# Retention with a gated linear unit: output stores on GpSimd's DMA queue, query loads on SyncE's

## The chip, the cores and the metric

The kernel runs on one core of one Trainium2 chip. A core has five engines that run side by side, each through its own instructions in order: TensorE (PE, matmuls and, as PEld, its weight loads), VectorE (DVE), ScalarE (ACT), GpSimd (POOL) and SyncE (SP, which here only issues transfers). Transfers between HBM and the on-chip memory (SBUF) run on 16 DMA engines; they are issued from SP, ACT or POOL. The metric is the device time of one execution in microseconds (us), lower is better.

## What is computed

Eight batches, eight heads, 576 tokens, head dimension 64, all inputs and the output in 32-bit floats:

```
scores = (q @ k^T) / sqrt(64)
ret    = (scores * Dmat) @ v             Dmat[i, j] = gamma_h^(i - j) for i >= j, else 0
x      = ret, heads side by side         8 x 576 x 512
gate   = sigmoid(sum_k conv_w[k] * x[t - 4 + k])     5 taps along the tokens, zeros before the start
out    = (gate * (x @ w_val)) @ w_out
```

## The kernel before

Tokens are taken in chunks of 128, so a batch has four full chunks and a tail of 64 tokens; the tails of two batches make one chunk. For each group of four batches there are sixteen full chunks and two tail chunks, 36 in all (`chunks`, numbered t). The decay is split into a factor for each token of v (`gin`) and one for each output token (`gout`), so that within a chunk a plain triangular mask suffices, and what earlier chunks contribute goes through a 64 x 64 state for each head.

The program is written out by hand as a loop over slots, t = -2 to 37 (line 419). The order of the lines in a slot is the order of instructions on each engine. A slot t

- issues the loads of chunk t + 6 on SP (`load`, lines 78 and 81: a 256 KB tile each of k and v, into 9 buffers each; a tail has its own q tile),
- casts to bf16 on POOL: v of chunk t + 2, multiplied by `gin` (`cast_v`, line 202), k of chunk t + 3 (`cast_k`, line 197), and one quarter of a batch's queries for the next slot (`cast_q`, line 215),
- on PE makes the scores of chunk t + 1 (line 260), the values of chunk t (line 301), transposes the keys of chunk t + 2 and that quarter of queries (line 222), and adds the carried part and the state's update of chunk t + 1 (lines 284 and 332); DVE masks the scores and copies the transposed keys out of PSUM (lines 269 and 230), ACT copies states and queries (lines 343 and 244),
- and does half of the second layer's unit n = t // 2 - 1, which is two chunks of x: an even slot does the convolution as matmuls (line 365), the sigmoid (ACT, line 373) and the value projection (line 380), an odd one the output projection (line 391), with ACT's copy of its result into `ob` (line 394, five buffers) and the store of it (lines 397 and 400).

So even slots are longer on PE than odd ones. From slot to slot the engines run apart as far as buffers allow: the bf16 tiles of k and v have four buffers each, those of q five.

A full batch's queries are loaded as one tile of 1 MB, `fqb`, of which line 215 casts a quarter (one remainder of the token number modulo 4) at a time. Batches 0 and 1 are loaded on SP at the start; batches 2 to 7 on POOL's queue, at the head of the slot that `qload` names, into three buffers. The quarters of batch b are cast in four slots that are placed backwards from the batch's first chunk (`qjobs`): for batches 2 to 7 the first of them is turned in slot 3, 7, 11, 17, 21 and 25, and cast one slot before that.

A store on SP waits for ACT's copy of its `ob`, and whatever SP has to load next waits behind it. The output weights are loaded as floats (`wof`, line 110) and cast to bf16 in slot 2: quarters 0 and 2 by DVE, 1 and 3 by ACT (line 190). The first output projection, in slot 3, is the first to need them.

The lines that the steps of the prediction follow:

```
for b in qload.get(t, []):           # line 438: query loads of a slot
    load_queries(b)
if t >= 0 and ok(t + LA - 2):        # line 440: k and v of chunk t + 6 on SP
    load(t + LA - 2)
```

Of the kernel before, what the change touches and what calls it, by code (L numbers as in the profile page):

```python
# [13 lines left out]
F32 = mybir.dt.float32  # L14
# [7 lines left out]
def kernel(  # L22
# [10 lines left out]
    nc = tc.nc  # L33
    B, H, S, D = q.shape
    DM = moe_w_val.shape[0]
    KC = moe_conv_w.shape[0]
    P = 128
    NP = H // 2
    NCH = S // P
    TAIL = S - NCH * P  # L40
    PAD = KC - 1
    GB = 4
    LA = 8
    RQ = NCH
# [5 lines left out]
    half = ctx.enter_context(tc.tile_pool(name="half", bufs=2))  # L50
# [13 lines left out]
    chunks = []  # L64
# [6 lines left out]
    with tc.manual_schedule():  # L71
# [13 lines left out]
        def load(t):  # L85
            kind, b, c = chunks[t]
            load_one("k", k, kind, b, c, LA + 1)
            if kind == "tail":
                load_one("q", q, kind, b, c, 2)
            load_one("v", v, kind, b, c, LA + 1)  # L90

        def load_queries(b):
            t = half.tile([P, H, RQ, D], F32, name="fqb", bufs=3)
            (nc.sync if b < 2 else nc.gpsimd).dma_start(out=t.rearrange("p h r d -> p h (r d)"),  # L94
                              in_=q[b, :, 0:RQ * P, :].rearrange("h (p r) d -> p h (r d)", r=RQ))
            loaded["qb", b] = t

# [85 lines left out]
        def prep_wv(copy, part):  # L183

            src = wvf.rearrange("p o (pr ab hl j) -> p o pr ab hl j", pr=2, ab=2, hl=2)
            for (blk, j0, ab, hl) in ((0, 0, 0, 0), (0, 64, 1, 0), (2, 0, 1, 1), (2, 64, 0, 1))[2 * part:2 * part + 2]:
                copy(wvb[:, :, blk:blk + 2, j0:j0 + 64], src[:, :, :, ab, hl, :])
# [7 lines left out]
        def cast_k(t):  # L195
            kb = bfp.tile([P, H, D], BF16, name="kb")
            (nc.vector if t < 2 else nc.gpsimd).tensor_copy(kb, loaded["k", *chunks[t]])  # L197
            kbf[t] = kb

        def cast_v(t):  # L200
            vb = bfp.tile([P, H, D], BF16, name="vb")
            nc.gpsimd.tensor_tensor(vb, loaded["v", *chunks[t]],  # L202
                                    gin[:, chunks[t][2], :].unsqueeze(2).to_broadcast([P, H, D]), op=ALU.mult)
            vbf[t] = vb
# [4 lines left out]
        def cast_q(job, eng=nc.gpsimd):  # L209
            qb = bfp.tile([P, H, D], BF16, name="qb", bufs=5)  # L210
            if job[0] == "own":
                src = loaded["q", *chunks[job[1]]]
            else:
                src = loaded["qb", job[1]][:, :, job[2], :]
            eng.tensor_copy(qb, src)  # L215
            qbf[job] = qb
# [10 lines left out]
        def turn_k(t):  # L227
            ps = turned(kbf[t])
            kt = tp_sb.tile([P, NP, P], BF16, name="kt")
            nc.vector.tensor_copy(kt, ps)  # L230
            ktd[t] = kt

        def turn_q(job, copy=nc.scalar.copy, pool=None):
            ps = turned(qbf[job], pool)
            if job[0] == "own":
                qt = tp_sb.tile([P, NP, P], BF16, name="qt")
                qtd["own", job[1]] = qt
                dst = qt
            else:
                b, r = job[1:]  # L240
                if r == 0:
                    qtd["batch", b] = tp_sb.tile([P, NP, RQ, P], BF16, name="qtb", bufs=2)
                dst = qtd["batch", b][:, :, r, :]
            copy(dst, ps)  # L244
# [21 lines left out]
        def masks(t, i):  # L266
            m = mask_q if chunks[t][0] == "full" else mask_t
            p = pp.tile([P, NP, P], BF16, name=f"p{i}")
            nc.vector.tensor_tensor(p, sps[t][i], m.unsqueeze(1).to_broadcast([P, NP, P]), op=ALU.mult)  # L269
            pt[t, i] = p  # L270
# [65 lines left out]
        def take_state(t):  # L336
            kind, b, c = chunks[t]
            if kind != "full":
                return
            s = sbl[b % GB] if c == NCH - 1 else sbd[c % 2]  # L340
            for i in range(2):
                r = slice(i * 64, i * 64 + 64)
                nc.scalar.copy(s[r, :, i * 64:i * 64 + 64], st[b][r, :, i * 64:i * 64 + 64])  # L343
            state[b] = s
# [41 lines left out]
        def project(n, i):  # L386
            kind, b, c = chunks[2 * n]
            last = n == NT // 2 - 1
            o = ps_g.tile([P, DM], F32, name="g")
            for j in range(NP):  # L390
                nc.tensor.matmul(o, lhsT=zsb[n, j // 2][:, j % 2, i * P:(i + 1) * P], rhs=wob[:, j, :],  # L391
                                 start=(j == 0), stop=(j == NP - 1))
            ob = op_sb.tile([P, DM], F32, name="ob")
            nc.scalar.copy(ob, o)  # L394
            if kind == "full":
                c0 = (c + i) * P
                nc.sync.dma_start(out=out[b, c0:c0 + P, :], in_=ob)
            else:
                for j in range(2):
                    (nc.scalar if last and j else nc.sync).dma_start(out=out[b + 2 * i + j, NCH * P:S, :], in_=ob[j * TAIL:(j + 1) * TAIL])  # L400


        ok = lambda t: 0 <= t < NT
# [9 lines left out]
        qload = {}  # L413
        for b in range(2, B):
            first = min(s for s in qjobs if ("batch", b, 0) in qjobs[s])
            qload.setdefault(max(0, first - LA + 4), []).append(b)

        v_copy, g_copy, s_copy = nc.vector.tensor_copy, nc.gpsimd.tensor_copy, nc.scalar.copy
        for t in range(-2, NT + 2):
            n = t // 2 - 1  # L420
            unit = 0 <= n < NT // 2
            odd = t % 2 == 1
            jobs = qjobs.get(t, [])
            if t == -2:

                cast_k(0)
                turn_k(0)
                for s in sbl:
                    nc.vector.memset(s, 0.0)
                for r in range(RQ):  # L430
                    cast_q(("batch", 0, r), nc.vector if r % 2 else nc.gpsimd)
                cast_v(0)
                for r in range(RQ):
                    turn_q(("batch", 0, r), s_copy if r % 2 else v_copy, ps_g if r < 3 else None)
                warm = consts.tile([P, 1], F32, name="warm")
                nc.scalar.activation(warm, lsc, AF.Sigmoid)
                continue
            for b in qload.get(t, []):
                load_queries(b)
            if t >= 0 and ok(t + LA - 2):  # L440
                load(t + LA - 2)
            if ok(t + 2) and t == -1:
                cast_k(t + 2)
            if ok(t + 2):
                cast_v(t + 2)
            if t == -1:
                prep_wv(g_copy, 0)
            if ok(t + 3):
                cast_k(t + 3)
            for job in qjobs.get(t + 1, []):  # L450
                cast_q(job)
            if ok(t):
                take_state(t)
            if ok(t + 1):
                scores(t + 1)
                masks(t + 1, 0)
            if ok(t):
                values(t)
                if not odd:
                    take_x(t)  # L460
            if ok(t + 1) and not odd:
                masks(t + 1, 1)
            if unit and not odd:
                conv(n)
                gate(n, 0)
                gate(n, 1)
            if ok(t + 2) and not 1 <= t <= 3:
                turn_k(t + 2)
            if ok(t) and odd:
                take_x(t)  # L470
            if ok(t + 1) and odd:
                masks(t + 1, 1)
            if t == -1:
                prep_conv_weights()
            early = jobs if not 1 <= t <= 3 else []
            if unit:
                project(n, 0) if odd else value(n, 0)
            for job in early:
                turn_q(job)
            if unit:  # L480
                project(n, 1) if odd else value(n, 1)
            if ok(t + 2) and 1 <= t <= 3:
                turn_k(t + 2)
                for i, job in enumerate(jobs):
                    turn_q(job, v_copy if i % 2 else s_copy)
            if ok(t + 1):
                carried(t + 1)
                update(t + 1)
            if -1 <= t <= 0:
                prep_diagonals(2 * t + 2)  # L490
                prep_diagonals(2 * t + 3)
            if t == 1:
                prep_wv(s_copy, 1)
            if t == 2:
                for o in range(NP):
                    prep_wo(s_copy if o % 2 else v_copy, o)
                nc.gpsimd.tensor_copy(mask_t, mask)
                nc.gpsimd.memset(mask_t[0:64, 64:128], 0.0)
# [29 lines left out]
```

## Time and profile before

| what | value |
|---|---|
| median of 3 runs | 185.16 us (185.05 to 185.59) |
| the profiled execution | 185.59 us |
| its span in the profile | 183.8 us |
| PE busy | 153.4 us (83%) |
| DVE, ACT, POOL busy | 122.8, 88.4, 86.9 us |
| bytes moved by DMA | 40.21 MB, mean 219 GB/s |
| stores of 256 KB on SP | 32 |
| query loads of 1 MB on POOL, on SP | 6, 2 |

The page gives, for the profiled execution, each engine's busy time, a row of digits for each engine over 40 slices of the span (tenths busy; PEclk is the clock granted to PE in tenths of full speed), the DMA queues, and the chain of waits that ended last. Queue q1 is that of the transfers issued by SP, q0 that of those issued by POOL. In the timeline, a bracket after an instruction is the idle time of its engine before it, and what ended it. The difference between the execution's 185.59 us and its span of 183.8 us lies outside the recorded instructions.

### The profile page before, as it was taken

To read this page: it belongs to the slowest core of one execution; us is meant where nothing else is said; L and a number is where in the kernel's file an instruction comes from. 1 tells how busy PE (TensorE), PEld (TensorE's weight loads), DVE (VectorE), ACT (ScalarE), POOL (GpSimd) and SP (SyncE) were. 2 spreads that over 40 slices of the span, in tenths; PEclk is the share of its full clock that TensorE was granted. 3 is DMA by queue.
4 is the path that set the end of the run, shared out by engine and by line. 5 is a ranking of instruction groups with operands and counts; after the bars stand their busy time and mean duration, and the time that the engine had idled before them with its cause. 6 is when DMAs were issued, how large, how long until landed. Compare 5 with 4: busy or idle time off the path is not lost.

```text
span 183.8 us, 5590 instructions
## 1 busy us (share of the span) xinstructions
PE 153.4 (83%) x2273; PEld 113.3 (62%) x2273; DVE 122.8 (67%) x229; ACT 88.4 (48%) x180; POOL 86.9 (47%) x125
## 2 busy tenths in 40 slices
PE   0277092554899999999999999999999999999990
PEld 0255081341586776868778686776868778687640
DVE  6568452179277767787776777767787777877420
ACT  6353221140455575565655455575565655554331
POOL 5349120994249454491467369448565434400000
PEclk9999999555599999999999999999999999999999
DMA  5999999999695999779989999999999978413024
GB/s 142 284 308 234 235 338 203 224 248 273 176 200 129 304 261 230 204 180 263 261 234 259 326 204 270 298 263 261 242 250 256 263 171 175 180 59 114 23 95 114
DMA packets 89351, 40.21 MB, mean 219 GB/s; under 512 B 80090, under 2 KB 82158, under 8 KB 89326
## 3 DMA queue, kind: packets, MB, share of 16 engines
q1 hardware_dynamic: 87504, 33.30, 76.7%
q0 software_dynamic: 1632, 6.29, 11.3%
q8 instruction: 17, 0.28, 0.7%
q10 hardware_dynamic: 190, 0.27, 0.6%
q14 instruction: 8, 0.07, 0.1%
HBM read 30.42 MB, written 9.44 MB: 217 GB/s over the span
## 4 chain that ended last, share of the span: by engine, by line
PE 74%; SPq 10%; DMA 6%; DVE 4%; ACT 1%; issue 1%; POOL 1%; ACTq 0%; DVEq 0%; POOLq 0%
PE g L391 17%; PE g L380 16%; PE g L365 11%; PE tps L222 11%; DMA fkc<-in_k_dram 6%; PE o L301 6%; PE s L260 6%; SPq L78 5%; PE st L332 4%; DVE wob L190 3%; SPq L110 3%; PE o L284 3%; SPq L94 2%; ACT qtb L244 1%; ACT ob L394 1%
## 5 line engine op out<-in xcount | busy, mean ns | idle before, releaser
L269 DVE TENSOR_TENSOR p<-s,maskq 128x512 bf16<-128x512 f32 x64 | 43.8, 684 | 16.3 <-PE s L260 16.1
L197 POOL CAST kb<-fkc 128x512 bf16<-128x512 f32 x34 | 20.7, 609 | 54.5 <-DMA fkc<-in_k_dram 24.2
L202 POOL TENSOR_TENSOR vb<-fvc,gin 128x512 bf16<-128x512 f32 x36 | 37.8, 1051 | 10.0 <-DMA fvc<-in_v_dram 7.0
L391 PE MATMUL g<-wob,z 128*128 128x512 bf16 x144 | 38.0, 393 | 4.3 <-DVE wob L190 4.0
L383 DVE TENSOR_TENSOR z<-gate,g 128x512 bf16<-128x512 f32 x36 | 24.7, 687 | 19.4 <-PE g L380 19.4
L380 PE MATMUL g<-xg,wvb 128*128 128x256 bf16 x288 | 36.7, 273 | 0.0
L394 ACT COPY ob<-g 128x512 f32<-128x512 f32 x36 | 21.1, 585 | 31.8 <-PE g L391 31.5
L373 ACT ACTIVATE gate<-g 128x512 f32<-128x512 f32 x36 | 19.5, 595 | 19.6 <-PE g L365 19.6
L380 PEld LDWEIGHTS <-wvb 128*128 128x128 bf16 x288 | 26.7, 98 | 3.2 <-issue 0.6
L222 PE MATMUL tps<-ident,kb 128*128 128x128 bf16 x144 | 15.5, 235 | 14.0 <-POOL kb L197 9.4
L343 ACT CAST sbd<-st 64x256 bf16<-64x256 f32 x48 | 17.6, 366 | 15.6 <-PE st L332 15.1
L365 PE MATMUL g<-xg,dg 64*64 64x256 bf16 x720 | 23.5, 273 | 0.0
L391 PEld LDWEIGHTS <-z 128*128 128x128 bf16 x144 | 13.0, 100 | 15.6 <-issue 5.8
L244 ACT COPY qtb<-tps 128x512 bf16<-128x512 bf16 x27 | 15.9, 588 | 13.3 <-PE tps L222 13.3
L230 DVE COPY kt<-tps 128x512 bf16<-128x512 bf16 x36 | 15.2, 423 | 9.9 <-PE tps L222 9.8
L311 DVE TENSOR_TENSOR xg<-o,gout 128x512 bf16<-128x512 f32 x32 | 21.7, 679 | 0.0
L222 PEld LDWEIGHTS <-kb 128*128 128x128 bf16 x144 | 8.9, 103 | 19.8 <-POOL kb L197 10.1
L215 POOL CAST qb<-fqb 128x512 bf16<-128x512 f32 x30 | 18.6, 628 | 4.1 <-DMA fqb<-in_q_dram 4.1
L365 PEld LDWEIGHTS <-dg 64*64 64x64 bf16 x720 | 18.5, 107 | 2.1 <-issue 0.6
L222 PEld LDWEIGHTS <-qb 128*128 128x128 bf16 x144 | 12.1, 108 | 10.7 <-POOL qb L215 3.9
L222 PE MATMUL tps<-ident,qb 128*128 128x128 bf16 x132 | 14.0, 234 | 2.9 <-ACT qtb L244 1.3
L301 PE MATMUL o<-p,vb 128*64 128x128 bf16 x288 | 15.8, 235 | 0.0
(59 smaller groups left out, 135.1 us busy)
## 6 DMA issues: line engine op xcount, KB each, us to landing
fkc<-in_k_dram SPq DMA_DIRECT2D x32, 256.0 KB, 5.3
fvc<-in_v_dram SPq DMA_DIRECT2D x32, 256.0 KB, 5.3
out_dram<-ob SPq DMA_DIRECT2D x32, 256.0 KB, 3.6
fqb<-in_q_dram POOLq DMA_DIRECT2D x6, 1024.0 KB, 8.1
fqb<-in_q_dram SPq DMA_DIRECT2D x2, 1024.0 KB, 10.1
wvf<-in_moe_w_val_dram SPq DMA_DIRECT2D x1, 1024.0 KB, 6.6
wof<-in_moe_w_out_dram SPq DMA_DIRECT2D x4, 256.0 KB, 5.8
fkc<-in_k_dram SPq DMA_DIRECT2D x8, 128.0 KB, 3.8
```

The costliest lines, as they stand in the source:

```text
L197: (nc.vector if t < 2 else nc.gpsimd).tensor_copy(kb, loaded["k", *chunks[t]])
L202: nc.gpsimd.tensor_tensor(vb, loaded["v", *chunks[t]], gin[:, chunks[t][2], :].unsqueeze(2).to_broadcast([P, H, D]), op=ALU.mult)
L222: nc.tensor.transpose(ps[:, pr, :], flat[:, pr * P:(pr + 1) * P], ident)
L269: nc.vector.tensor_tensor(p, sps[t][i], m.unsqueeze(1).to_broadcast([P, NP, P]), op=ALU.mult)
L301: nc.tensor.matmul(o[r, pr, :], lhsT=vb[:, 2 * pr + i, :], rhs=pt[t, i][:, pr, :], start=(fresh and pr == 0), stop=(pr == NP - 1), skip_gr ...
L311: nc.vector.tensor_tensor(by_token(x[:, bl, :, PAD + i0:PAD + i0 + P]), ops[t].rearrange("p o (r n) -> p o n r", r=RQ), by_token(gout[:, : ...
L365: nc.tensor.matmul(g[bank][cols, pr, :], lhsT=dg[rows, blk, kk, :], rhs=xs(n, rows, blk, kk), start=(pr == 0 and kk == 0), stop=(pr == 1 a ...
L373: nc.scalar.activation(t, gps[n][i], AF.Sigmoid)
L380: nc.tensor.matmul(vps[:, j, :], lhsT=wvb[:, o, 2 * i + j, :], rhs=xs(n, slice(0, P), o, PAD), start=(j == 0 and o == 0), stop=(j == 1 and ...
L383: nc.vector.tensor_tensor(z, gsb[n][i], vps, op=ALU.mult)
L391: nc.tensor.matmul(o, lhsT=zsb[n, j // 2][:, j % 2, i * P:(i + 1) * P], rhs=wob[:, j, :], start=(j == 0), stop=(j == NP - 1))
L394: nc.scalar.copy(ob, o)
```

## The change

All query loads are issued on SP, in two buffers instead of three, and from batch 2 on two slots sooner (`qload` subtracts 6 instead of 4, though not below slot 0): in slots 0, 1, 5, 11, 15 and 19 instead of 0, 3, 7, 13, 17 and 21. Load b takes the buffer of batch b - 2, and waits on SP until its last quarter has been cast.

The stores of all units but the last move from SP to POOL's queue. The projection puts them into a list, and the next slot issues them on POOL, after its three casts: each stands behind the casts of v for chunk t + 2, of k for chunk t + 3 and of the queries, and ahead of the casts of the following slot. The last unit's stores stay where they were, on SP and ACT. In the order of the built program SP's queue after chunk 5's values is: the queries of batch 2, k and v of chunk 6, the queries of batch 3, k and v of chunk 7, and on. POOL's queue then carries 36 stores: 32 of 256 KB and, of the first pair of tail chunks, four of 128 KB. The order on PE, DVE and ACT is the same as before.

```diff
         def load_queries(b):
-            t = half.tile([P, H, RQ, D], F32, name="fqb", bufs=3)
-            (nc.sync if b < 2 else nc.gpsimd).dma_start(out=t.rearrange("p h r d -> p h (r d)"),
+            t = half.tile([P, H, RQ, D], F32, name="fqb", bufs=2)
+            nc.sync.dma_start(out=t.rearrange("p h r d -> p h (r d)"),
                               in_=q[b, :, 0:RQ * P, :].rearrange("h (p r) d -> p h (r d)", r=RQ))
...
             nc.scalar.copy(ob, o)
+            if last:
+                for j in range(2):
+                    (nc.scalar if j else nc.sync).dma_start(out=out[b + 2 * i + j, NCH * P:S, :], in_=ob[j * TAIL:(j + 1) * TAIL])
+            else:
+                ready.append((n, i, ob))
+
+        ready = []
+
+        def store(n, i, ob):
+            kind, b, c = chunks[2 * n]
             if kind == "full":
                 c0 = (c + i) * P
-                nc.sync.dma_start(out=out[b, c0:c0 + P, :], in_=ob)
+                nc.gpsimd.dma_start(out=out[b, c0:c0 + P, :], in_=ob)
             else:
                 for j in range(2):
-                    (nc.scalar if last and j else nc.sync).dma_start(out=out[b + 2 * i + j, NCH * P:S, :], in_=ob[j * TAIL:(j + 1) * TAIL])
+                    nc.gpsimd.dma_start(out=out[b + 2 * i + j, NCH * P:S, :], in_=ob[j * TAIL:(j + 1) * TAIL])
...
-            qload.setdefault(max(0, first - LA + 4), []).append(b)
+            qload.setdefault(max(0, first - LA + 2), []).append(b)
...
             for job in qjobs.get(t + 1, []):
                 cast_q(job)
+            while ready:
+                store(*ready.pop(0))
             if ok(t):
                 take_state(t)
```

## The prediction

> **What bounds the kernel now.** I read the page first, then busy time by stage, then the chain of waits in order of time, then the timeline of the first 50 us.
>
> ```profile
> span 183.8 us, 5590 instructions
> ...
> PE   0277092554899999999999999999999999999990
> ...
> POOL 5349120994249454491467369448565434400000
> PEclk9999999555599999999999999999999999999999
> DMA  5999999999695999779989999999999978413024
> ```
>
> ```profile
> 57.61:167.55 109.94, 109.94 (x1760) 83.13 (x1761) 83.56 (x142) 62.64 (x134) 57.90 (x78) 1.00 0.92 231
> 28.80:32.60 3.80, 0.00 (x0) 0.00 (x0) 0.69 (x1) 0.00 (x0) 0.65 (x2) 1.00 0.91 175
> 39.80:43.80 4.00, 0.05 (x2) 0.08 (x1) 4.00 (x2) 0.00 (x0) 3.69 (x6) 0.50 1.05 312
> 43.80:49.80 6.00, 5.45 (x28) 2.69 (x27) 2.53 (x5) 2.00 (x4) 0.38 (x1) 0.50 0.88 191
> ```
>
> Columns of the second view: stretch, its length, busy us of PE, PE loads, DVE, ACT, POOL, then PE clock, DMA share, GB/s. From 57.6 to 167.6 PE is busy all 109.94 us, 14 pairs of slots of 7.85 us each. Nothing taken off SP, POOL or DMA can shorten that; a feed that comes late can lengthen it. What can be won lies before 50 us: PE stands still for 3.8 and 4.0 us, and its clock is at half from 32.7 to 49.8.
>
> ```profile
> 20.66 11.15 DMA fkc<-in_k_dram
> 31.95 0.61 POOL kb L197
> ...
> 38.27 5.52 DVE wob L190
> 43.83 3.57 PE g L391 x8
> ```
>
> ```profile
> 15.95 1.06 POOL L94 DMA_DIRECT2D fqb<-in_q_dram  x1
> ...
> 26.59 1.04 POOL L202 TENSOR_TENSOR vb<-fvc,gin 128x512 bf16<-128x512 f32 x1 [3.76 <-DMA fvc<-in_v_dram]
> ...
> 31.95 0.61 POOL L197 CAST kb<-fkc 128x512 bf16<-128x512 f32 x1 [4.32 <-DMA fkc<-in_k_dram]
> ...
> 38.27 5.85 DVE L190 CAST wob<-wof 128x512 bf16<-128x512 f32 x2
> ...
> 42.46 1.03 POOL L202 TENSOR_TENSOR vb<-fvc,gin 128x512 bf16<-128x512 f32 x1
> ```
>
> The first pause ends with the cast of chunk 4's keys (31.95), whose load was late. The second ends with DVE's casts of the output weights.
>
> **Part 1: the query load of batch 2 leaves the head of the queue.** POOL issues it at 15.95, while the loads that PE waits for are still queued on SP. The DMA queues between 22 and 26 us (packets, MB, share):
>
> ```profile
> q0 software_dynamic: 256, 0.98, 75.9%
> q1 hardware_dynamic: 531, 0.31, 29.2%
> ```
>
> POOL's queue (q0) moved 0.98 of its 1.05 MB there, SP's (q1) only 0.31. In 36 to 40 us, when SP's queue had the engines to itself, it moved 227 GB/s (mean of 239, 216, 215, 239), which is 1.15 us for a 256 KB tile; 0.31 MB would have taken 1.4 us, not 4. So q0 cost SP's loads 2.6 us here, and up to 1.05 MB / 0.34 = 3.1 us in all (0.34 MB/us is the rate at 23 to 25 us). In the changed program's SP order this load stands behind chunk 5's values, so chunk 4's keys come 3.1 us sooner and PE starts at 29.5 instead of 32.62. Bounds: 2.6 to 3.8 (the whole pause). **I take 3.1.**
>
> **Part 2: what POOL does while DVE casts wob.** Two rows:
>
> ```profile
> L190 DVE CAST wob<-wof x2: 411/2962/5512, 38.3 to 43.7; 128x512 bf16<-128x512 f32 x2
> L94 POOL DMA_DIRECT2D fqb<-in_q_dram x6: 922/922/1060, 15.9 to 112.3; - x6
> ```
>
> One cast took 0.41 us, the other 5.51. POOL ran casts without a gap from 31.95 to 43.49 and DVE came free 0.2 us later: DVE was held until POOL paused. The Trainium skill, "SBUF — State Buffer", section "Who interferes with whom", says the same, that VectorE's casts and GpSimd share a port pair and the loser waits whole instructions; the row goes further, since DVE was held over eight POOL instructions in a row, not one. After the change POOL must pause sooner. Its run from chunk 4's keys to chunk 5's keys takes 4.4 us (31.95 to 36.35), so it ends at 28.85 + 4.4 = 33.3. The next instruction, the cast of batch 2's first queries, waits for the load moved in part 1: v3 lands at 23.4 (26.5 less 3.1), batch 1's 1 MB adds 3.1, four tiles 4.6, batch 2's 1 MB 3.1, so 34.2 to 35.0. DVE reaches wob 6.3 us after chunk 4's keys (31.95 to 38.27), at 35.2, or up to 1.3 sooner at full PE clock (five groups of transposes, 0.27 each). So DVE comes at 33.8 to 35.2 into a POOL pause of 33.3 to 35.0. If it gets in, PE's 3.98 us wait at line 391 goes. Bounds 0.8 (DVE misses the pause and waits for POOL's next one, rival A) to 4.0. **I take 4.0**, since the early end of DVE's window fits.
>
> **Part 3: the clock.** The clock's row fell to 0.50 at 32.7 after the 3.8 us pause, and rose at 49.8 after six busy us. With pauses under 1 us it need not fall. Eight matmuls of line 391 took 3.57 us there and 1.73 at 150 us (1.84 saved); the transposes, carried, update and score groups at 0.6 instead of 0.33 add some 3. Bounds 0 to 5. **I take 3.0**, nearer the upper row, as no 3 us pause is left.
>
> The Trainium skill, "TensorE: Matmul & The Clock Gate", "What's actually happening", has the clock drop after one idle window of about 3.4 us; by that rule, as an estimate, the whole 5 would be saved here.
>
> **Part 4: 36 stores move from SP to POOL, six loads from POOL to SP.** POOL pays 0.92 for a 1 MB load's issue (row above); SP's issues of the same stores take 0.33 at the least, 0.38 in the median. So a store costs POOL 0.33 to 1.06, taken 0.92. Per pair of slots POOL has two v multiplies (1.05), two k casts (0.61), two q casts (0.61): 4.54, and with two stores 6.4 of 7.85. The store waits for the copy of the slot before; behind it in POOL's queue stand the casts of slots t+1 and t+2. Its data is there at about 0.1 us into slot t; 1.9 for both issues and 1.7 for v and k put chunk t+4's keys at 3.7, needed by the transpose in slot t+2 at 9.7. Six us of cover: cost 0. The last stores keep their queues; the ones before come some 8 us ahead of the end.
>
> SP no longer waits for output copies:
>
> ```profile
> SPq L397 <- ACT ob L394: 26.0, 10, 6.5
> ```
>
> PE was full, so this saves nothing itself, but it fills DMA gaps such as 54.5 to 57.5. With two buffers, load b waits for the casts of batch b-2, and k and v loads stand behind it. In the worst case (batch 6, issued in slot 15, waiting for slot 15's cast) chunk 21's keys follow 3.1 + 1.15 later and are needed three slots (11.8 us) on: cost 0. But demand is tight: four tiles 4.6, half a query load 1.5 and two stores 1.5 make 7.6 of 7.85 us per pair, so PE starting nine us sooner must be fed from former gaps. Chunk 7's keys now stand behind two query loads (34.6 + 2.3 + 3.1 + 1.2 = 41.2), and PE wants them near 43. Bounds 0 to 3 given back; **I take 1.0.**
>
> **Sum.** 3.1 + 4.0 + 3.0 - 1.0 = 9.1. The profiled execution took 185.59 us (span 183.8 and 1.8 around it), 0.43 above the median of 185.16. 185.59 - 9.1 = 176.5; against the median, **176.1 us**.
>
> **Rivals.**
>
> A. *DVE is caught again.* If batch 2's queries are cast before DVE's second cast starts, POOL runs on until chunk 7's keys are missing: 34.6 plus 4.4 of casts is 39.0, wob is done at 39.8 instead of 44.1. Gain 4.3, clock as before: 180.9 us. For it: the two windows overlap by about half. Against: a first cast that slips in leaves only 0.4 us to fit.
>
> B. *The feed gives it all back.* The two early query loads on SP delay chunks 7 to 9 and the gaps aren't refilled: PE stops near 43 and 55 us. Gain 0 to 2: 184. Against: before, POOL's key casts at 49.4 and 54.3 us waited for PE, not for a load, so the feed was ahead there.
>
> C. *POOL becomes the bound (slower).* Stores on POOL's queue hold it longer than a load's issue does. POOL is the bound from (7.85 - 4.54) / 2 = 1.65 us a store, and the start's gain is eaten from 1.94. At 2.3, some 16 pairs x 1.29 = 20.6 lost, 9.1 won: 196.7. For it: POOL's multiply beside the issue at 15.95 took 1.31 instead of 1.05, so generation may cost beyond its row. Against: the issue row, with eight times the rows of a store.
>
> The Trainium skill, "DMA: Bandwidth & Descriptors", "Issuing engine by pattern", speaks against this change: simple stores belong on Sync, whose issue is generally faster. Its fixed cost of about 2.0 us per GpSimd DMA ("Anatomy of one DMA"), if it held POOL, would make an estimate of 8.5 per pair, 11 us lost over 16 pairs and 187 in the sum; the row of 0.92 says that it doesn't hold POOL.
>
> **How the numbers follow.** Forecast 50% (own range 173.5 to 178.5), A 28%, B 8%, C 12%, no visible change 2%. Range: lower end with all of the clock and nothing given back, 173.0; upper end past A, 182.5. What a measurement can tell from no change is about 0.3%. Faster: forecast, A and most of B, 83%; same 4%; slower 13%.
>
> **What would show it.** Right: the cast of chunk 4's keys near 28.8; wob's casts 0.4 us each; line 391's first matmul near 35; PEclk without its four fives; L407 issues near 0.9 us; PE full from 45 us on. Wrong: wob's cast still long (A); PE idle behind POOL's kb casts in mid-run, released by DMA (B) or by POOL's stores (C).

## The result and the profile after

| | before | after |
|---|---|---|
| median | 185.11 us (184.83 to 185.59, 4 runs) | 178.22 us (176.82 to 179.26, 4 runs) |
| the profiled execution | 185.59 us | 178.59 us |
| its span | 183.8 us | 176.4 us |
| PE busy | 153.4 us | 151.0 us |
| POOL busy | 86.9 us | 100.2 us |

The change made the kernel faster: the ratio is 0.962, with a 95% interval of 0.955 to 0.969. In this section and the next a median is over all runs of a kernel, while a ratio leaves disturbed runs out, so that the two need not agree to the last digit.

Lines of the page of the changed kernel:

```profile
span 176.4 us, 5547 instructions
...
PE   0165559498999999999999979999999999999980
...
POOL 5084234572993499841696099749978737612200
PEclk9999999969999999999999999999999999999998
DMA  5979999899999899999998999999999989313124
```

The four fives of the clock's row have become one six. PE is full some two slices earlier than before, and a new dent stands in slice 23 (a 7), which the kernel before did not have. Slice 23 begins at 101 us. These are the two places where PE stood still before (start and duration in us, the bracket being the idle time before):

```profile
32.62 0.55 PE L222 MATMUL tps<-ident,kb 128*128 128x128 bf16 x4 [3.86 <-POOL kb L197]
...
43.83 3.57 PE L391 MATMUL g<-wob,z 128*128 128x512 bf16 x8 [3.98 <-DVE wob L190]
```

The timeline of the changed kernel there, PE's and then POOL's:

```profile
28.52 1.92 PE L380 MATMUL g<-xg,wvb 128*128 128x256 bf16 x16
30.27 0.39 PE L222 MATMUL tps<-ident,kb 128*128 128x128 bf16 x4
...
36.81 2.68 PE L391 MATMUL g<-wob,z 128*128 128x512 bf16 x8
```

```profile
28.83 0.61 POOL L197 CAST kb<-fkc 128x512 bf16<-128x512 f32 x1 [3.32 <-DMA fkc<-in_k_dram]
29.39 2.29 POOL L215 CAST qb<-fqb 128x512 bf16<-128x512 f32 x4
31.63 1.04 POOL L202 TENSOR_TENSOR vb<-fvc,gin 128x512 bf16<-128x512 f32 x1
32.62 0.61 POOL L197 CAST kb<-fkc 128x512 bf16<-128x512 f32 x1
36.24 0.61 POOL L215 CAST qb<-fqb 128x512 bf16<-128x512 f32 x1 [3.01 <-DMA fqb<-in_q_dram]
```

The groups of lines 222 and 391 carry no bracket any more: PE waits for neither. Chunk 4's keys are cast at 28.83 instead of 31.95. POOL's run of casts ends at 33.2 and the next begins at 36.24, so that DVE, which comes to the output weights at 35.40, finds POOL idle. One row by source line says what that is worth (least, median and longest duration in ns, then first and last start):

```profile
L190 DVE CAST wob<-wof x2: 416/418/420, 35.4 to 35.7; 128x512 bf16<-128x512 f32 x2
```

That was 411/2962/5512 before. The first projection begins at 36.81 instead of 43.83. The group of score matmuls (line 260) that stands at 54.14 before stands at 45.41 after, 8.73 us sooner, and from there on both kernels do the same work on a full PE. The lead does not last, though. This is the chain of waits near the dent:

```profile
91.74 2.12 SPq L94
93.86 0.04 issue
93.91 7.66 DMA fkc<-in_k_dram
...
101.69 0.62 POOL kb L197
...
102.36 0.40 PE tps L222 x4
```

SP issues batch 6's query load (from 90.62, in the chain from 91.74) and chunk 21's keys behind it at 93.91, which land 7.66 us later; POOL casts them at 101.69, and PE has then stood still for 1.00 us. The stretch that was full before (us, its length, busy us of PE, PE loads, DVE, ACT and POOL, clock, DMA share, GB/s) shows it as well:

```profile
57.61:167.55 109.94, 108.94 (x1752) 82.07 (x1745) 81.02 (x140) 60.15 (x127) 69.73 (x104) 1.00 0.91 226
```

PE lacks that one microsecond here; before it was busy for 109.94 of 109.94. PE's last projection group starts 7.67 us sooner than before (169.99 against 177.66), the span is 7.4 us shorter, and the execution 7.0.

### The profile page after: what moved, and what is told of

It is laid out like the page before. It is cut to its first block, busy times and chain, and to the rows that moved or that the text cites. A ratio compares the mean times of both kernels' runs of the same rounds, so it can differ in the third digit from the quotient of the medians.

```text
span 176.4 us, 5547 instructions
## 1 busy us (share of the span) xinstructions
PE 151.0 (86%) x2273; PEld 112.0 (63%) x2273; DVE 117.4 (67%) x229; ACT 88.4 (50%) x180; POOL 100.2 (57%) x155
## 4 chain that ended last, share of the span: by engine, by line
PE 59%; SPq 16%; DMA 11%; POOL 5%; issue 3%; ACT 2%; DVE 1%; ACTq 0%; POOLq 0%; DVEq 0%
PE g L391 14%; PE g L380 13%; PE g L365 9%; DMA fkc<-in_k_dram 8%; PE tps L222 8%; SPq L78 6%; PE o L301 5%; PE s L260 5%; SPq L94 4%; SPq L81 3%; SPq L110 3%; DMA fvc<-in_v_dram 3%; PE st L332 3%; PE o L284 2%; POOL qb L215 2%
## 5 line engine op out<-in xcount | busy, mean ns | idle before, releaser
L391 PE MATMUL g<-wob,z 128*128 128x512 bf16 x144 | 37.1, 386 | 0.3 <-DVE z L383 0.3
L394 ACT COPY ob<-g 128x512 f32<-128x512 f32 x36 | 21.1, 585 | 27.9 <-PE g L391 27.7
L407 POOL DMA_DIRECT2D out_dram<-ob x32 | 18.0, 564 | 14.4 <-ACT ob L394 13.4
L365 PE MATMUL g<-xg,dg 64*64 64x256 bf16 x720 | 24.0, 277 | 0.0
L222 PEld LDWEIGHTS <-qb 128*128 128x128 bf16 x144 | 11.3, 103 | 12.4 <-POOL qb L215 5.1
L222 PE MATMUL tps<-ident,qb 128*128 128x128 bf16 x132 | 13.0, 222 | 3.3 <-DVE kt L230 1.5
```

What stands on the lines that cost most here:

```text
L222: nc.tensor.transpose(ps[:, pr, :], flat[:, pr * P:(pr + 1) * P], ident)
L365: nc.tensor.matmul(g[bank][cols, pr, :], lhsT=dg[rows, blk, kk, :], rhs=xs(n, rows, blk, kk), start=(pr == 0 and kk == 0), stop=(pr == 1 a ...
```

## The experiments

My theory after the result: all of the gain comes from batch 2's load leaving the head of the DMA queue, which brings chunk 4's keys sooner and opens a gap in POOL's casts for DVE; the stores on POOL are neutral; and what is lost again at 101 us is lost to the feed. The rivals were that the stores or the buffers have a share in the gain or in the loss.

Twelve kernels were run. For each profile I read two numbers: how far PE is ahead of the kernel before at the score group of 54.14 us ("lead early"), and at the start of the last projection group (177.66 before, "lead at the end"). What lies between them was lost in mid-run. Both are read from one execution of each kernel, which in e8, e10 and e12 was the slowest of its kernel and in e4 the second slowest.

| kernel | median us (lowest to highest) | ratio, 95% interval | lead early | lead at the end | lost |
|---|---|---|---|---|---|
| changed | 178.22 (176.82 to 179.26) | 0.962 (0.955 to 0.969) | 8.73 | 7.67 | 1.06 |
| e1: before, batch 2's load on SP | 178.57 (177.04 to 181.20) | 0.960 (0.954 to 0.967) | 10.32 | 8.99 | 1.33 |
| e2: before, stores on POOL | 184.23 (182.97 to 186.33) | 0.992 (0.989 to 0.996) | 1.25 | 1.25 | 0 |
| e3: before, output weights cast on ACT | 180.12 (179.57 to 180.31) | 0.971 (0.967 to 0.975) | 5.92 | 5.92 | 0 |
| e4: changed, three buffers | 182.08 (178.30 to 184.54) | none | 8.97 | 3.47 | 5.50 |
| e5: changed, once more | 179.06 (177.25 to 181.63) | 0.958 (0.954 to 0.963) | 9.13 | 8.58 | 0.55 |
| e6: changed, queries two slots later | 177.90 (176.93 to 179.58) | 0.963 (0.958 to 0.967) | 9.64 | 8.20 | 1.44 |
| e7: e6, output weights loaded later | 178.65 (176.94 to 180.68) | 0.963 (0.959 to 0.968) | 11.95 | 8.85 | 3.10 |
| e8: changed, five spare casts on POOL | 181.56 (180.07 to 184.47) | 0.979 (0.973 to 0.984) | 9.67 | 1.44 | 8.23 |
| e9: before, spare matmuls in the pauses | 183.04 (182.64 to 183.53) | 0.992 (0.988 to 0.995) | 2.18 | 2.18 | 0 |
| e10: changed, twelve spare casts on POOL | 178.10 (177.75 to 182.13) | 0.964 (0.961 to 0.968) | 3.66 | 3.66 | 0 |
| e11: changed, no stores | 176.22 (175.37 to 177.75) | 0.956 (0.950 to 0.961) | 9.75 | 9.75 | 0 |
| e12: e7, no stores | 174.05 (172.77 to 176.11) | 0.941 (0.935 to 0.947) | 9.76 | 9.76 | 0 |

The kernel before, beside them on the same chip: median 185.51 with e1 to e4, 184.98 with e5 to e8, 184.73 with e9 to e12.

### e1: the one load alone

```diff
-            (nc.sync if b < 2 else nc.gpsimd).dma_start(out=t...
+            (nc.sync if b < 3 else nc.gpsimd).dma_start(out=t...
```

> The kernel before with one edit: batch 2's query load is issued on SP behind chunk 5's values instead of on POOL; all else as before. Theory (the gain of the change comes from this one load): chunk 4's keys are cast near 28.8 us, wob's two casts on DVE take 0.42 us each, the first projection starts near 36.8 instead of 43.8, and the time is 177 to 179.5 us. Rival (SP freed of its waits for output copies brings the gain): no more than 1.5 us won, 183.6 us or more.

Measured: 178.57 us, as fast as the whole change. By source line, and in PE's timeline:

```profile
L190 DVE CAST wob<-wof x2: 418/628/837, 35.2 to 35.5; 128x512 bf16<-128x512 f32 x2
```

```profile
100.83 0.40 PE L222 MATMUL tps<-ident,kb 128*128 128x128 bf16 x4 [1.05 <-POOL kb L197]
```

DVE's casts are short (the second, which waited for one query cast of POOL, took 0.84 us), and even the pause near 101 us is there, though all stores are still on SP, the buffers are three and the other five loads are still on POOL. So one of the eight query loads makes the gain, and neither the stores on POOL nor the two buffers make the loss.

### e2: the stores alone

The changed kernel with the query loads as before (three buffers, six on POOL, their old slots).

> The kernel before with the other half of the change: the stores go to POOL's queue as in the changed kernel, the query loads stay on POOL in three buffers. Theory: the start is untouched (PE waits near 28.8 and near 39.9 us as before) and PE was full behind it, so 184.5 to 186 us; a store's issue takes POOL 0.54 us. Rival (the stores bring the gain): 178 to 182 us. Second rival (POOL with both kinds of issue becomes late): over 187 us.

Measured: 0.9924 (0.9888 to 0.9959), 0.4 to 1.1% faster. By source line:

```profile
L190 DVE CAST wob<-wof x2: 828/2572/4315, 38.4 to 42.7; 128x512 bf16<-128x512 f32 x2
```

The start is as before, with a cast of 4.3 us, and PE waits 2.78 us at line 391 instead of 3.98. POOL's busy time went from 86.9 to 105.8 us at no cost to PE. The small gain is that of the early lead, 1.25 us; that the stores themselves bring it was not separated from a start that differs from one execution to the next. It goes with a shorter hold, 4.3 us instead of 5.5: DVE's cast ended at 42.74, between these two casts of POOL, which follow each other without a break:

```profile
41.85 0.60 POOL L197 CAST kb<-fkc 128x512 bf16<-128x512 f32 x1
42.41 0.80 POOL L215 CAST qb<-fqb 128x512 bf16<-128x512 f32 x1
```

### e3: the hold on DVE alone

```diff
-                    prep_wo(s_copy if o % 2 else v_copy, o)
+                    prep_wo(s_copy, o)
```

> The kernel before with one edit: all four casts of the output weights on ACT, none on DVE. Theory (DVE was held by POOL's run of casts, and that alone cost PE 3.98 us): the wait at the first projection goes, chunk 4's keys are as late as before (31.9 us), and the time is 180.5 to 181.7 us. Rival (the projection would have waited for something else there, the weights' load or the masks on DVE): less than 1 us won, 184 us or more.

Measured: 180.12 us, 5.4 us under the median beside it and a shade better than expected. The clock's row is nearly whole:

```profile
PEclk9999999957999999999999999999999999999999
```

ACT casts all four parts by 38.6 us and PE's wait on DVE is gone, while the load of batch 2 stands where it was. So the two causes of the late start can be had apart: the hold, with the half clock that followed, is the larger part. This kernel also has the narrowest spread of those that gain more than 2 us, 0.7 us.

### e4, e5, e6: is the loss at 101 us made by buffers or by order?

Three buffers again (e4: `bufs=2` to `bufs=3`), the changed kernel unaltered (e5), and the query loads two slots later (e6: `first - LA + 2` to `first - LA + 4`).

> The changed kernel with three buffers for the query batches instead of two, so that SP's load of batch 6 no longer waits for batch 4's last cast. Theory (that wait made chunk 21's keys late, cast at 101.69 us, and cost PE its 1.06 us pause there): PE has no pause between 57 us and the end, and the median is 1 us or so under that of the changed kernel, 177 us. Rival (the DMA engines are short of throughput with PE 8.7 us ahead): a pause of 0.5 us or more stays, near the tail chunks or chunk 21, and 178 us or more.

> The changed kernel once more, unedited, to stand beside the two versions that go with it. 176.8 to 179.3 us, as in its first four times, with PE pausing some 1 us for chunk 21's keys near 101 us. Theory (the DMA feed decides that pause): its length differs from one execution to the next with the rate that the DMA engines reach, which is why its times spread over 2 us while the kernel before spreads over less. Rival: the spread comes from the start, where DVE's casts are held in some executions.

> The changed kernel with the query loads from batch 3 on placed two slots later in SP's queue (in the slots that the kernel before used), still in two buffers. Theory (batch 6's 1 MB stood ahead of chunk 21's keys in a queue that is short of throughput): chunk 21's keys land some 3 us sooner, the pause near 101 us goes, PE is full from 42 us on, and the median falls by about 1 us, to 177. Rival (the queue is short whatever stands in front): PE pauses for another load within the next ten us, and the median stays within 0.5 us of the changed kernel's.

e4's runs scatter too far for a ratio, and its profiled execution took 182.58 us, so the size of its pause is not typical; that there is one bears on the question. POOL's timeline, then PE's:

```profile
103.10 0.61 POOL L197 CAST kb<-fkc 128x512 bf16<-128x512 f32 x1 [4.64 <-DMA fkc<-in_k_dram]
```

```profile
103.77 0.61 PE L222 MATMUL tps<-ident,kb 128*128 128x128 bf16 x4 [2.64 <-POOL kb L197]
```

With a third buffer the same keys are late all the same, and PE's clock falls behind them. e1 has three buffers too, and its profiled execution, of 177.04 us, paused 1.05 us for them. My theory, that SP's wait for a buffer made chunk 21's keys late, fell. Moving the queries back (e6) moved the pause and did not remove it; PE's timeline of e6:

```profile
93.99 0.40 PE L222 MATMUL tps<-ident,kb 128*128 128x128 bf16 x4 [1.38 <-POOL kb L197]
```

e5 shows how much chance is in it: the same program as the changed one lost 0.49 us at 101.45 in its profiled execution instead of 1.00. Of its six executions three took 177.25 to 177.58 us and three 180.54 to 181.63. The latter left no trace, so the rival named for the spread, a hold on DVE in some executions, stays open. In the one that did leave a trace, POOL's query cast began before DVE's second cast, and that one still took no more than 0.86 us:

```profile
L190 DVE CAST wob<-wof x2: 415/636/858, 34.8 to 35.2; 128x512 bf16<-128x512 f32 x2
```

```profile
35.12 0.62 POOL L215 CAST qb<-fqb 128x512 bf16<-128x512 f32 x1 [3.05 <-DMA fqb<-in_q_dram]
35.68 0.48 POOL L509 COPY maskt<-mask 128x128 bf16<-128x128 bf16 x1
```

### e7: win more at the start

e6, with the output weights' loads behind those of chunk 4, so that chunk 4's keys need not wait for them.

```diff
         wo_src = moe_w_out.rearrange("(pr ab hl p) n -> ab hl p pr n", pr=2, ab=2, hl=2)
+        load(3)
+        load_queries(1)
+        load(4)
         for (p0, blk, ab, hl) in ((0, 0, 0, 0), (64, 0, 1, 0), (0, 2, 1, 1), (64, 2, 0, 1)):
             nc.sync.dma_start(out=wof[p0:p0 + 64, blk:blk + 2, :], in_=wo_src[ab, hl])
-        load(3)
-        load_queries(1)
-        for t in range(4, LA - 2):
+        for t in range(5, LA - 2):
             load(t)
```

> The version with the later query loads, and the four loads of the output weights moved behind chunk 4's values at the start. Theory of the start (PE's waits until 36 us are for loads in the order of SP's queue, and these four stand 4.3 us ahead of chunk 3's keys although nothing needs them before 35 us): chunk 3's keys are cast near 19 us instead of 23.3 and chunk 4's near 25, PE gets 2 to 4 us further ahead by 45 us. If the feed behind it holds, 174 to 175.5 us; if the feed is the bound from there on, the pauses grow by what was won and the time is that of the version without this edit, 177.

The early lead grew from 9.64 to 11.95 us, and the time did not fall. PE's timeline (line numbers are higher by one in this kernel):

```profile
51.37 0.40 PE L223 MATMUL tps<-ident,kb 128*128 128x128 bf16 x4 [0.39 <-POOL kb L198]
...
67.51 0.40 PE L223 MATMUL tps<-ident,kb 128*128 128x128 bf16 x4 [0.22 <-POOL kb L198]
...
93.22 0.40 PE L223 MATMUL tps<-ident,kb 128*128 128x128 bf16 x4 [2.17 <-POOL kb L198]
```

Three pauses on late keys, 2.78 us, take it back. At the end e7's lead (8.85) is that of e1 (8.99) and e5 (8.58): in the traces without a longer pause the loads let PE keep 7.7 to 9 us of what it wins early.

### e8 and e10: is DVE held by POOL?

Spare casts on POOL behind chunk 5's key cast, meant to close the gap that the change opened: five in e8, twelve in e10.

```diff
...
             if ok(t + 3):
                 cast_k(t + 3)
+            if t == 2:
+                for i in range(12):
+                    nc.gpsimd.tensor_copy(spare[i % 5], wvf[:, i % NP, :])
             for job in qjobs.get(t + 1, []):
                 cast_q(job)
```

> The changed kernel with five more casts of 128x512 on POOL (copies of value weights into tiles that nothing reads) behind the cast of chunk 5's keys, so that POOL is busy in the 3 us in which it waited for batch 2's queries. Theory (a run of POOL instructions without a gap holds DVE's cast of the output weights): the first of DVE's casts takes 4 to 5 us, the first projection starts near 40.5 us instead of 36.8, and the time is 181 to 183 us. Rival (DVE was held by something else before the change, the load of the weights or the state of the queues): DVE's casts take 0.42 us each as in the changed kernel, 178 us.

e8 missed: the five casts ended too soon. Its rows by source line and in POOL's timeline (line numbers higher by one, in e10 too):

```profile
L191 DVE CAST wob<-wof x2: 494/501/508, 35.8 to 36.3; 128x512 bf16<-128x512 f32 x2
```

```profile
32.41 2.85 POOL L463 CAST spare<-wvf 128x512 bf16<-128x512 f32 x5
35.44 0.61 POOL L216 CAST qb<-fqb 128x512 bf16<-128x512 f32 x1 [0.18 <-DMA fqb<-in_q_dram]
36.00 0.48 POOL L513 COPY maskt<-mask 128x128 bf16<-128x128 bf16 x1
```

The spare casts end at 35.26 and POOL pauses 0.18 us; DVE's casts start at 35.8, when POOL is busy again, and take 0.50 us each: the first ended at 36.33, behind POOL's query cast (to 36.06), though POOL's copy follows that one without a break. So DVE can get in between two instructions of POOL. The time that e8 lost was lost to late keys in mid-run, with pauses of 1.64 us at 86.61 and 3.77 at 105.91, and is no evidence on what a hold costs.

> The changed kernel with twelve spare casts on POOL behind chunk 5's key cast, in place of five in the run above, so that POOL has no gap from about 28.8 to some 39.5 us and DVE comes to the output weights in mid-run. Theory (DVE is held until POOL pauses): the first or second of DVE's two casts lasts until POOL's first gap, 3 us or more, and line 391 starts near 39 to 40 us. Rival (DVE gets in between any two POOL instructions): 0.4 to 0.7 us each, line 391 starts at 36.5 to 37.5 or waits for a query cast and not for the weights. The row decides, not the time, which also holds what POOL's later casts lose.

With twelve spare casts POOL has no gap. POOL's timeline, the row by source line, and PE's timeline of e10:

```profile
32.21 6.77 POOL L463 CAST spare<-wvf 128x512 bf16<-128x512 f32 x12
38.91 0.63 POOL L216 CAST qb<-fqb 128x512 bf16<-128x512 f32 x1
39.47 0.31 POOL L513 COPY maskt<-mask 128x128 bf16<-128x128 bf16 x1
39.84 0.30 POOL L514 MEMSET maskt<- 64x64 bf16 x1
```

```profile
L191 DVE CAST wob<-wof x2: 1286/3078/4870, 35.2 to 40.0; 128x512 bf16<-128x512 f32 x2
```

```profile
40.11 1.01 PE L392 MATMUL g<-wob,z 128*128 128x512 bf16 x2 [3.68 <-DVE wob L191]
```

DVE's first cast starts at 35.19, in mid-run, and lasts 4.87 us, to 40.06; POOL's first break after 27.9 lies between the copy that ends at 39.78 and the memset at 39.84. PE waits 3.68 us for it, much as it did before the change. So the hold is shown: beside a POOL that runs without a gap DVE's cast can last several of its instructions. Its end is tied to POOL's: in every trace where one of these casts took longer than its usual 0.42 us, it ended 0.28 or 0.29 us behind the end of an instruction of POOL (at 43.78 behind 43.49 before the change, 42.74 behind 42.45 in e2, 40.06 behind 39.78 here). What is not shown is which instruction lets DVE in. The first cast here, like those before the change and in e9, came through at a break in POOL's run; but in e2, e5 and e8, and in the second cast here (1.29 us, to 41.27, behind POOL's multiply, which ended at 40.98), POOL's next instruction followed without one.

This profiled execution took 182.13 us, the slowest of e10's four; the other three took 177.75 to 178.42. Their spans (175.3 to 176.7 us against 180.4) and granted clocks (0.986 to 1.000 against 0.967) speak for it that DVE was not held for long in them, beside the same spare casts. Only one execution has a trace, so that isn't shown.

### e9: what the half clock cost

The kernel before, with 40 spare matmuls on PE in each of its two pauses; the waits stay.

```diff
...
+            if t == 3:
+                keep_busy(40)
             if unit:
                 project(n, 0) if odd else value(n, 0)
...
+            if t == 2:
+                keep_busy(40)
             if ok(t + 2) and 1 <= t <= 3:
                 turn_k(t + 2)
```

> The kernel before, with 40 spare matmuls put into each of PE's two early pauses (ahead of the transposes of chunk 4's keys and ahead of the first output projection), so that PE has work while it waits; the waits themselves stay. Theory (part 3 of the prediction, the clock): the granted clock stays at 1.0 or falls for one short stretch, line 391's first eight matmuls take near 1.75 us instead of 3.57, the wait for the output weights stays, and the time falls by 2 to 3 us, to 182.0 to 183.0. Rival (the half clock lay in stretches where PE waited for copies in any case): the clock's row is mended, the time stays within 0.5 us of before's.

The clock's row, and PE's timeline at the first projection:

```profile
PEclk9999999969999999999999999999999999999999
```

```profile
39.37 3.24 PE L228 MATMUL tps<-ident 128*128 128x128 bf16 x40
42.45 0.59 PE L396 MATMUL g<-wob,z 128*128 128x512 bf16 x2
44.59 1.46 PE L396 MATMUL g<-wob,z 128*128 128x512 bf16 x5 [1.54 <-DVE wob L190]
```

The wait for DVE's weights stays (the cast still ends at 44.53), and what comes after it runs at the full clock. In the profile PE is 2.18 us ahead, although chunk 4's keys came 0.74 us later than in the profile before (cast at 32.69). By the times it is 0.8% (0.5 to 1.2), or 0.9 to 2.1 us of 184.73, more than the rival's 0.5 us, and mostly less than the 2 to 3 that were expected.

### e11 and e12: without the stores

The changed kernel and e7, both without the output stores of all units but the last.

```diff
-            while ready:
-                store(*ready.pop(0))
+            ready.clear()
```

> The changed kernel without the output stores, all but those of the last unit: 36 transfers of 256 KB or less are left out, and their issues on POOL. Theory (what gives part of the gain back is the DMA feed): PE is full from 57 us on, no pause near 101 us; the end comes 8.7 us ahead of before's, so the time is 176.5 to 177.3, and its spread falls below 1 us. Rival (the pause comes from the order of the queues, not from their throughput): a pause near 101 us stays, 178 to 179, spread as it was.

> The kernel with the queries two slots later and the output weights' loads behind chunk 4's values, again without the output stores but those of the last unit. With the stores it won 3 us at the start and lost them in three pauses. Theory (DMA feed): the pauses go and the 3 us stay, 173.0 to 174.5. Rival (order): the pauses stay, 176.5 to 178.5.

The pauses in mid-run are gone from both: the lead is the same at the end as early, 9.75 and 9.76 us. The stretch that showed the loss, in e11:

```profile
57.61:167.55 109.94, 109.07 (x1715) 82.50 (x1728) 81.08 (x140) 60.92 (x127) 51.92 (x71) 1.00 0.70 153
```

The 0.87 us that PE seems to lack here are no pause: the trace holds 2255 of the program's 2273 matmuls, and the view of waits names no wait of PE over 0.2 us between 41 and 165 us. DMA moves 153 GB/s here instead of 226. e12 keeps what e7 lost, 174.05 us against 178.65. In its profiled execution (176.11 us, the slowest, left out of the ratio) the start is no better than e11's, because PE waits for batch 2's queries:

```profile
37.78 0.61 PE L223 MATMUL tps<-ident,qb 128*128 128x128 bf16 x4 [2.37 <-POOL qb L216]
```

One part of the expectation missed. e11's times still spread over 2.4 us, where I expected less than 1: the start differs from run to run as well, not the mid-run alone.

### What they say together

The "lost" column sorts itself. With the stores in place, a kernel that is up to 5.92 us ahead loses nothing (e2, e3, e9, e10), and each one that is 8.73 us ahead or more loses between 0.55 and 8.2 (in e4 and e8 a dip of the clock behind the pauses is part of it). Without the stores, 9.75 us ahead loses nothing. So the loss goes with the traffic of the stores: PE ahead of its old schedule by more than 6 to 9 us asks for keys sooner than the DMA engines bring them beside 9.4 MB of stores. Nothing tried here beat the changed kernel clearly while computing the same: e6's 177.90 lies within the spread.

## Why the prediction was right, point by point

Direction, size and range held: 176.1 was predicted, 173.0 to 182.5 the range, and 178.2 measured. Against its own profile the forecast was a gain of 9.1 us, and 7.0 came.

- **Part 1, the load off the queue's head: 3.1 predicted.** The keys came 3.12 us sooner, cast at 28.83 where 28.85 was worked out. PE's step was mis-sized: "PE starts at 29.5 instead of 32.62" took for granted that PE was free by then. It was busy with line 380 until 30.3 in this execution, so it started at 30.27, 2.35 us sooner. (Chunk 3's keys had been cast at 23.34 instead of 22.22, and the convolution behind them took 2.08 us instead of 1.52.) In e10, whose keys were cast at 27.87, PE still started only at 30.07. The bound of this step is PE's own work, not the load.
- **Part 2, DVE and POOL: 4.0 predicted.** The wait of 3.98 us went whole. POOL's run ended at 33.2 (33.3 predicted), DVE came at 35.40 (33.8 to 35.2), and POOL's next cast at 36.24 (34.2 to 35.0): both later than thought, in the order that was hoped for. DVE's second cast ended at 36.15, 0.09 us ahead of POOL. e3 and e10 show that the hold was the right reason for the wait, but the rule drawn from one row, "DVE was held until POOL paused", is too strict, and that row was misread: between 38.27 and 43.49 POOL ran seven instructions, not eight, and before them, from 37.29 to 38.21, it issued a load, beside which e9's first cast on DVE took its usual 0.42 us. In e5, the same program, and in e1, e4 and e11 POOL's query cast began before DVE's second cast, which is rival A's condition, and DVE still got in behind that one instruction (0.84 to 0.86 us). So the gap of 3.0 us let the first cast through, and A failed also because a busy POOL does not always hold DVE. What A foretold came in e10's profiled execution, of 182.13 us, where A said 180.9.
- **Part 3, the clock: 3.0 predicted.** In the profile it is 2.4: 0.69 between the first transposes and the first projection (36.81 is 7.02 sooner, less 2.35 and 3.98), and 1.71 from there to the score group (8.73 less 7.02). One slice at 0.6 was left: from 35.02 to 38.42 us the clock was at half, though no pause of PE between 28.5 and 35 us was over 0.96 us, so "with pauses under 1 us it need not fall" was no safe ground. With the same four pauses e1 kept the full clock from 29 us on, and its early lead is 10.32. e9, which mends the clock alone, gives 2.2 in its profile (2.9 with the 0.74 by which its keys came later) and 0.9 to 2.1 by the times. By the rule of the Trainium skill that the prediction quoted ("TensorE: Matmul & The Clock Gate", "What's actually happening") all 5 us, as an estimate, were to be had; neither run shows more than 2.9.
- **Part 4, the stores on POOL: 0 predicted, 0 found.** A store's issue holds POOL for 0.54 us, not for the 0.92 that was taken from a load of four times the size:

```profile
L407 POOL DMA_DIRECT2D out_dram<-ob x32: 539/544/738, 44.9 to 167.0; - x32
```

  The price was too high and the cover was ample either way, so rival C never came near its 1.65 us a store. e2 and e1 show it from both sides. The estimate of 187 us, which let the Trainium skill's fixed cost of a GpSimd DMA ("DMA: Bandwidth & Descriptors", "Anatomy of one DMA") hold POOL in full, does not fit this case: the stores alone gave 184.23 and cost PE nothing. What POOL pays for them is a wait of its own behind ACT's copies, 13.4 us by the view of waits, with nothing late behind it:

```profile
POOL out_dram L407 <- ACT ob L394: 13.4, 6, 5.0
```

- **Part 4, the feed: 1.0 predicted, 1.06 found in the profile, but in another place.** It was expected near 43 and 55 us; PE was full there, and the pause came at 102 us, in the very stretch (batch 6's load, chunk 21's keys) that was costed at nothing. So that the size fits is luck. That sum gave the keys 11.8 us of cover counted in slots and 4.25 us of delay, and left out that PE's lead uses up what the queue had in hand. The pause was not SP's wait for a buffer either, as e4 and e1 show. And it isn't a fixed cost: it was 0.49 us in e5's execution of the same program, whose times in both series run from 176.8 to 181.6. Rival B named the right mechanism and overrated it: it takes back 1 of 9 us, not all.
- **The rest.** Some 0.3 us was lost behind the last projection and 0.4 outside the span. With 0.75 from part 1, 0.6 from part 3 and 0.06 from the feed these make up the 2.1 us between 9.1 and 7.0.

Still open: what decides whether DVE gets in between two instructions of POOL, what came of it in the executions without a trace (e5, e10), and how the early start comes to differ by a microsecond between executions of one program.

## What to carry to other kernels

A large load issued from another engine's queue can hold up small ones that matter more, so look at what stands in front of the first tile that the bottleneck lacks: here one of eight loads was worth all of the gain. When an elementwise instruction takes ten times its usual duration, look at what the neighbouring engine ran beside it, and move the work to another engine (as in e3) or to a time when the neighbour stands still. And before adding up gains at the start of a streaming kernel, ask how far ahead the loads can follow: here 6 us were free, and from 8.7 on some of what was won early was lost again later.

## What was not expected of the hardware

The hold on DVE is no matter of one instruction: one cast lasted 5.51 us over seven instructions of POOL before the change, 4.3 over five in e2 and 4.87 over nine in e10. Each time it ended 0.28 or 0.29 us behind the end of one of POOL's instructions, at a break in POOL's run (0.06 us in e10) or without one (e2). Beside a POOL that stood still the same cast took 0.42 us; where it got in behind the first instruction of POOL that ended, 0.49 to 1.29 us. DVE holds POOL in turn: in e2 POOL's query cast, in front of which DVE got in, took 0.80 us instead of 0.61.

A 256 KB store from POOL's queue took 4.4 us from issue to landing (median of 32), against 3.6 from SP's, and a store's issue held POOL for 0.54 us, where that of a 1 MB load had held it for 0.92.
